# A gated mix of linear attention and a token MLP on one core: eight accumulators in the first stage, bias columns turned on VectorE, w2's second half moved in the load queue, kv in four column groups

## The chip, the cores and the metric

The kernel runs on one core of one Trainium2 chip. The metric is the device time of one execution in microseconds (us). Before the change it is 163.13 us, the median of three runs from 163.01 to 163.31.

## What is computed

The input x has 2048 rows (tokens) of 512 features, all arrays are bf16. With 32 heads of 16 features the reference is, cut to what matters:

```python
qkv = (x @ wqkv) split into q, k, v per head
phi = lambda t: where(t > 0, t + 1, exp(t)) + 1e-6
pq, pk = phi(q), phi(k)
kv  = einsum("bhsd,bhse->bhde", pk, v)          # 16x16 per head
den = einsum("bhqd,bhd->bhq", pq, pk.sum(over s)) + 1e-6
a   = (pq @ kv / den) @ wo
h   = layernorm(x)                              # over the features
u   = gelu(einsum("bsd,sf->bdf", h, w1) + b1)   # mixes tokens, 2048 -> 1792
b   = (einsum("bdf,fs->bds", u, w2) + b2), transposed
g   = sigmoid((x * gate_w).sum(-1))
out = g * a + (1 - g) * b
```

The output is divided through by the gate: with odds = exp(x . gate_w), out = (odds * a + b) / (1 + odds), so both halves can be summed in one accumulator.

## The kernel before, in words

The tokens are 16 tiles of 128 rows (t), the features 4 blocks of 128 (k, j), the hidden width of the MLP 14 blocks of 128 (NF). PSUM is one pool of eight banks, each 128x512 in fp32; every accumulator takes one. TensorE's order is the order of the program, and so are SP's queue, VectorE's and ScalarE's instructions that stand in `pin` or `keep_in_program_order`.

1. **Start** (lines 133 to 186). SP's queue loads x and the first part of w1 (w1A, one row block per token tile) in turns. ScalarE's queue loads the bias rows (b1 as 14 rows, b2 as 16) and the first 128 columns of w1A. TensorE runs 18 warm-up products of ones and then turns the bias rows into columns with an identity matrix (vps); ScalarE copies these out at t = 1 (L229, L230).
2. **Stage one** (L216 to L277). VectorE does the LayerNorm of a tile and TensorE multiplies it into NFA = 7 accumulators accA, row block after row block; the last four row blocks are done accumulator by accumulator, so that ScalarE can apply gelu to each. VectorE then does the gate sums of 12 tiles (L253).
3. **k** (L314). For each tile four matmuls k = x wk, phi on ScalarE and VectorE (L280), and, four tiles behind, four matmuls that sum G = x^T phi(k) in four banks (g_step). VectorE adds up z, the sum of phi(k), beside that.
4. **The mixed stage** (L469 to L491). Seven more blocks of the MLP's first layer (accB, from w1's second part w1B) stand between the q-tiles (L347), the block-diagonal kv product (kv_blocks, L416) and its product with wo (w2_blocks, L436). z makes a way through DRAM: zp_dram, transposing loads, a reduction (z_row), zr_dram, and back to all partitions (z_mixed); z_order puts it in order in zb.
5. **Normalisation** (normalise, L388). Per tile VectorE multiplies phi(q) by z, reduces, inverts and scales by odds and the inverse, in four operations. SP stores the tile in q_dram; after each four tiles, turn (L408) loads them back transposed into pqT, 512 columns, in four transposing loads (one per feature block).
6. **Output** (L538 to L556). For 8, then 4, then 3 tiles TensorE first sums the MLP's second layer into held accumulators yps (y_mm, 14 matmuls of w2h and uT) and then adds the attention part (a_mm, four matmuls of pqT and W2sb); finish scales by 1/(1+odds) and adds the bias on ScalarE, and SP stores. The last tile is done in 384 and 128 columns, the first on VectorE, the last on ScalarE.

w2 comes in two halves of 1024 columns. Half 0 takes the place of w1A (wpool has two equal buffers), half 1 that of w1B, which is read until the last accB matmul. Each of SP's loads and stores is issued when its data and its place are there and all before it in SP's queue have been issued:

```python
for t in range(12):
    normalise(t)              # ends with: store tile t to q_dram
    if t == 3:
        for f0, f1 in ((0, 3), (3, 7), (7, 10), (10, NF)):
            load_w2(1, f0, f1 - f0)
    if t % 4 == 3:
        turn(t // 4)          # four transposing loads of these four tiles
```

Before a transposing load of q_dram is issued, the four stores that it reads must have landed.

Of the kernel before, what the change touches and what calls it, by code (L numbers as in the profile page):

```python
# [7 lines left out]

ACT = mybir.ActivationFunctionType
ALU = mybir.AluOpType  # L10
# [1 line left out]
BF16 = mybir.dt.bfloat16  # L12
# [4 lines left out]
def kernel(  # L17
# [13 lines left out]
    nc = tc.nc  # L31
    P = nc.NUM_PARTITIONS
# [7 lines left out]
    S, D = X.shape  # L40
    F = B_w1.shape[1]
    NT = S // P
    ND = D // P
    NF = F // P
    SC = 512
    NSC = S // SC
    assert S == 2048 and D == 512 and F == 1792
    NFA = NF // 2
    FA = NFA * P
    TAIL = 4  # L50

# [5 lines left out]
    b1_view = B_b1.rearrange("(f p) -> f p", p=P)  # L57
    b2_view = B_b2.rearrange("(t p) -> t p", p=P)
    gw_row_view = gate_w.rearrange("(o d) -> o d", o=1)

    persist = ctx.enter_context(tc.tile_pool(name="persist", bufs=1))
    wpool = ctx.enter_context(tc.tile_pool(name="wstream", bufs=2))
    work = ctx.enter_context(tc.tile_pool(name="work", bufs=3))
    dpool = ctx.enter_context(tc.tile_pool(name="dpool", bufs=1, space=bass.MemoryType.DRAM))
    psum = ctx.enter_context(tc.tile_pool(name="psum", bufs=8, space=bass.MemoryType.PSUM))
# [1 line left out]
    def ptile(shape, dt, name):  # L67
        return persist.tile(shape, dt, name=name, tag=name)

    def bank(name):  # L70
        return psum.tile([P, SC], FP32, name=name, tag="bank")

    def mm(o, lhsT, rhs, start, stop, **kw):
        tc.keep_in_program_order(
            nc.tensor.matmul(o, lhsT=lhsT, rhs=rhs, start=start, stop=stop, **kw)  # L75
        )
# [5 lines left out]
    wk_sb = ptile([P, ND, D], BF16, "wk_sb")  # L82
    wv_sb = ptile([P, ND, D], BF16, "wv_sb")
    wo_sb = ptile([P, ND, D], BF16, "wo_sb")
    pqT = ptile([P, ND, S], BF16, "pqT")
    uT = ptile([P, NF, D], BF16, "uT")
    G_sb = ptile([P, ND, D], BF16, "G_sb")
    kvbdT = ptile([P, ND, P], BF16, "kvbdT")
    pq = ptile([P, NT, D], BF16, "pq")
    zb = ptile([P, D], FP32, "zb")  # L90
# [2 lines left out]
    prod = ptile([P, NH, HEAD + 1], FP32, "prod")  # L93
    W2sb = ptile([P, ND, D], BF16, "W2sb")
    mask = ptile([P, P], BF16, "mask")
    ident = ptile([P, P], BF16, "ident")
    gw_b = ptile([P, D], BF16, "gw_b")
    b_rows = ptile([NF + NT, P], BF16, "b_rows")
    b1_sb = ptile([P, NF], FP32, "b1_sb")
    b2_sb = ptile([P, NT], FP32, "b2_sb")  # L100
    mv = ptile([P, NT, nc.vector.BN_AGGR_DIM], FP32, "mv")
# [11 lines left out]
    eps_t = ptile([P, 1], FP32, "eps_t")  # L113

    nc.vector.memset(eps_t[:], EPS)


    w1A = wpool.tile([P, NT, FA], BF16, name="w1A", tag="w")
    w1B = wpool.tile([P, NT, FA], BF16, name="w1B", tag="w")

    pin = tc.keep_in_program_order

    def load(o, i, eng=None, **kw):
        pin((eng or nc.sync).dma_start(out=o, in_=i, **kw))  # L124

    def load_x(t0, t1):
        load(xr[:, t0:t1, :], x_view[:, t0:t1, :])

    def load_w1a(t):
        load(w1A[:, t, :], w1_view[:, t, 0:FA])  # L130


    tbl = work.tile([P, 1], FP32, name="tbl", tag="tbl", bufs=2)
    load(b_rows[0:NF, :], b1_view, nc.scalar)
    load(w1A[:, 0, 0:P], w1_view[:, 0, 0:P], nc.scalar)
    load(b_rows[NF : NF + NT, :], b2_view, nc.scalar)
    pin(nc.scalar.activation(out=tbl[:], in_=eps_t[:], func=ACT.Sqrt))

    load_x(0, 1)
# [2 lines left out]
    for t in range(1, NT):  # L142
        if t + 1 < NT:
            load_x(t + 1, t + 2)
        load_w1a(t)
    load(gw_b[:], gw_row_view.to_broadcast([P, D]))
    load(wk_sb[:], wqkv_view[:, :, D : 2 * D])
    for c in range(NSC):
# [11 lines left out]
    for j in range(ND):  # L160
# [4 lines left out]
    load(wq_sb[:], wqkv_view[:, :, 0:D])  # L165


    make_identity(nc, ident[:])
    nc.gpsimd.memset(mask[:], 0.0)
    nc.gpsimd.affine_select(  # L170
        out=mask[:], in_=mask[:], compare_op=ALU.is_gt, fill=1.0,
# [3 lines left out]
        out=mask[:], in_=mask[:], compare_op=ALU.is_ge, fill=0.0,  # L175
# [6 lines left out]
    one = nc.const_aps.tensor(1.0, [P, 256], BF16)  # L182
    for _ in range(18):
        mm(warm_ps[:, :256], one[:, 0:P], one, True, True)
    vps = bank("vps")
    mm(vps[:, : NF + NT], b_rows[:], ident[0 : NF + NT, 0 : NF + NT], True, True)

    BS = nc.vector.BN_STATS_DIM  # L190
# [2 lines left out]
    def ln_bn(t, d0, d1, h, parts):  # L193
        if h == 0:
            stats[t] = work.tile([P, parts, BS], FP32, name="stats", tag=f"stats{parts}", bufs=4)
        pin(nc.vector.bn_stats(out=stats[t][:, h, :], in_=xr[:, t, d0:d1]))  # L196
# [9 lines left out]
    def ln_apply(t):  # L206
        pin(nc.vector.reciprocal(out=rstd[:, t : t + 1], in_=sd[:, t : t + 1]))
        pin(
            nc.vector.tensor_scalar(
                out=xh[:, t, :], in0=xr[:, t, :],  # L210
                scalar1=mv[:, t, 0:1], scalar2=rstd[:, t : t + 1],
                op0=ALU.subtract, op1=ALU.mult,
            )
        )
# [4 lines left out]
    for t in range(1, NT):  # L219
        if t < HALVES:  # L220
            ln_bn(t, 0, D // 2, 0, 2)
            ln_apply(t - 1)
            ln_bn(t, D // 2, D, 1, 2)
        else:
            ln_bn(t, 0, D, 0, 1)
            ln_apply(t - 1)
        ln_aggr(t)
        if t == 1:
            pin(nc.scalar.copy(out=b1_sb[:], in_=vps[:, :NF]))  # L229
            pin(nc.scalar.copy(out=b2_sb[:], in_=vps[:, NF : NF + NT]))  # L230
    ln_apply(NT - 1)


# [31 lines left out]

    accA = [bank("accA") for _ in range(NFA)]

    def mlp1(acc, w, col, t, last):
        mm(acc[:], w[:, t, col : col + P], xh[:, t, :], t == 0, last)

    for t in range(NT - TAIL):
        for j in range(NFA):
            mlp1(accA[j], w1A, j * P, t, False)
    for j in range(NFA):
        for t in range(NT - TAIL, NT):
# [49 lines left out]
    def evict(o, acc, i):  # L325
        if i % 2 == 0:
            pin(nc.scalar.copy(out=o, in_=acc))
        else:
            pin(nc.vector.tensor_copy(out=o, in_=acc))

    for i in range(ND):
        evict(G_sb[:, i, :], Gps[i][:], i)
    pin(nc.vector.tensor_copy(out=z_parts[:, 0, :], in_=zacc[:]))
# [2 lines left out]
            out=z_parts[:, 1, :], in0=zacc[:], in1=z_parts[:, 0, :], op=ALU.subtract  # L336
# [4 lines left out]
    def mlp1_block(j):  # L341
        acc = bank("accB")
        for t in range(NT):
            mlp1(acc, w1B, (j - NFA) * P, t, t == NT - 1)
        return acc
# [70 lines left out]
    def kv_blocks():  # L416
        kvps = bank("kvps")
        for j in range(ND):
            for k in range(ND):
                for p in range(0, P, 64):  # L420
                    c = j * P + p
                    mm(kvps[p : p + 64, j * 64 : j * 64 + 64], wv_sb[:, k, c : c + 64],
                       G_sb[:, k, c : c + 64], k == 0, k == ND - 1, tile_position=(0, p))

        for j in range(ND):
            for p in range(0, P, 32):
                r = (p + 32 * j) % P
                pin(
                    nc.vector.tensor_tensor(
                        out=kvbdT[r : r + 32, j, p : p + 32],  # L430
                        in0=kvps[p : p + 32, j * 64 + p % 64 : j * 64 + p % 64 + 32],
                        in1=mask[p : p + 32, p : p + 32], op=ALU.mult,
                    )
                )
# [12 lines left out]
    w2s = []  # L447

    def load_w2(h, f0, n=7):
        if f0 == 0:  # L450
            w2s.append(wpool.tile([P, NF, S // 2], BF16, name="w2h", tag="w"))
        load(
            w2s[h][:, f0 : f0 + n, :],
            w2_view[:, f0 : f0 + n, h * (S // 2) : (h + 1) * (S // 2)],
        )
# [10 lines left out]
    gates = [[], [12, 13], [14, 15], []]  # L466
    qi = 0
    waiting = []
    for b in range(NFA):  # L469
        acc = mlp1_block(NFA + b)  # L470
        waiting.append((acc, NFA + b))
        if b == 0:
            kv_blocks()
        if b == 1:
            w2_blocks()
        if b < QB:
            for _ in range(n_q[b]):
                q_tile(qi)
                qi += 1
            for t in gates[b]:  # L480
                gate(t)
            if b == 2:
                gate_odds(0, NT)
            if b == 1:
                z_row()
        if b == QB - 1:
            z_order()
        if b >= QB - 1:
            for a, j in waiting:
                gelu(a, j)  # L490
            waiting = []  # L491
# [7 lines left out]

    for t in range(12):  # L500
        normalise(t)
        if t == 3:
            for f0, f1 in ((0, 3), (3, 7), (7, 10), (10, NF)):
                load_w2(1, f0, f1 - f0)
        if t % 4 == 3:
            turn(t // 4)
# [12 lines left out]

    def finish(t, yps, d0, d1):  # L520
        ot = work.tile([P, D], BF16, name="ot", tag="ot", bufs=6)
        if t < NT - 1 or d1 == D:
            pin(
                nc.scalar.activation(  # L524
                    out=ot[:, d0:d1], in_=yps[:, d0:d1], func=ACT.Identity,
                    scale=c1[:, t : t + 1], bias=c2[:, t : t + 1],
                )
            )
        else:
            pin(  # L530
                nc.vector.tensor_scalar(  # L531
                    out=ot[:, d0:d1], in0=yps[:, d0:d1], scalar1=c1[:, t : t + 1],
                    scalar2=c2[:, t : t + 1], op0=ALU.mult, op1=ALU.add,
                )
            )
        load(o_view[:, t, d0:d1], ot[:, d0:d1])
# [14 lines left out]
    t = NT - 1  # L551
# [35 lines left out]
```

## Time and profile before

| what | value |
|---|---|
| median of the runs | 163.13 us |
| the profiled execution | 163.22 us |
| its span, first to last instruction | 161.5 us |
| granted TensorE clock | 1.0 |
| TensorE, VectorE, ScalarE busy | 98%, 73%, 33% |
| 128x512 matmul of accB, busy for 16 | 3.45 us |
| HBM read, written | 19.28 MB, 4.46 MB |

The profile is of one execution. Its times count from the start of the span, and the 1.7 us between span and execution time lie outside it. Matmuls are pipelined: a matmul's own duration (379 ns for 512 columns) is longer than the 0.216 us from one start to the next. The chain of waits goes back from the last instruction, at each step to what released it. "Landing" is the moment at which a transfer has signalled its end; SP's line shows only the time in which it issues. All loads and stores that this document speaks of go through queue q1 (SP's) but for those issued by ScalarE, which go through q10.

### The profile page before, as it was taken

Reading aid. Unit: us, or ns where it says so; the run is one execution under the profiler, and the core shown is the slowest. Engines: PE = TensorE matmul, PEld = TensorE weight load, DVE = VectorE, ACT = ScalarE, POOL = GpSimd, SP = SyncE. Lnnn points to the kernel's source line nnn. Section 1 sums busy time; section 2 is a strip of 40 time slices with the busy share of each in tenths; the row PEclk is TensorE's granted clock in tenths of the full one; section 3 lists DMA queues with packets and bytes.
Section 4 is the critical chain, followed back from the end, with each engine's and each line's share of the span. In section 5 each row is a group of like instructions: output and inputs, shape, how many; then the busy total and the mean of one; then the engine's idle time right before and its main releaser. Section 6 shows DMA issues by size and latency. Waiting matters only on the chain.

```text
span 161.5 us, 2209 instructions
## 1 busy us (share of the span) xinstructions
PE 157.6 (98%) x789; PEld 72.9 (45%) x789; DVE 117.1 (73%) x271; ACT 53.6 (33%) x92; POOL 1.6 (1%) x10
## 2 busy tenths in 40 slices
PE   7999999999999999999999999999999999999992
PEld 5344444444444445444444444444444444444452
DVE  2899989999999996998959999999999900000001
ACT  4222248962342124261448720000008321150041
POOL 3000000000000000000000000000000000000000
PEclk9999999999999999999999999999999999999999
DMA  4999996445799742179930103999565367260021
GB/s 129 277 349 354 320 234 130 99 101 106 236 394 375 188 131 81 38 210 383 332 65 0 38 33 85 318 396 299 159 79 162 80 187 252 65 180 19 0 97 32
DMA packets 36838, 28.33 MB, mean 175 GB/s; under 512 B 20444, under 2 KB 33116, under 8 KB 36828
## 3 DMA queue, kind: packets, MB, share of 16 engines
q1 hardware_dynamic: 36352, 27.90, 58.7%
q10 hardware_dynamic: 476, 0.30, 0.6%
q8 instruction: 6, 0.10, 0.3%
q14 instruction: 4, 0.03, 0.1%
HBM read 19.28 MB, written 4.46 MB: 147 GB/s over the span
## 4 chain that ended last, share of the span: by engine, by line
PE 94%; DMA 3%; SPq 1%; ACT 0%; issue 0%; ACTq 0%
PE yps L75 39%; PE accB L75 15%; PE accA L75 14%; PE qacc L75 9%; PE Gps L75 9%; PE kacc L75 9%; DMA w1A<-in_B_w_dram 3%; SPq L124 1%; PE kvps L75 0%; ACT ot L524 0%; PE w2ps L75 0%; ACTq L524 0%
## 5 line engine op out<-in xcount | busy, mean ns | idle before, releaser
L75 PE MATMUL yps<-uT,w2h 128*128 128x512 bf16 (+2 forms) x238 | 49.2, 366 | 0.0
L75 PEld LDWEIGHTS <-w2h 128*128 128x128 bf16 x238 | 22.8, 98 | 25.9
L524 ACT ACTIVATE ot<-yps,c,c 128x512 bf16<-128x512 f32 (+1 forms) x16 | 12.0, 758 | 50.0 <-DVE pq L400 24.4
L75 PE MATMUL accB<-xh,w1B 128*128 128x512 bf16 x112 | 25.0, 379 | 0.0
L75 PE MATMUL accA<-xh,w1A 128*128 128x512 bf16 x112 | 24.5, 379 | 0.2 <-DMA w1A<-in_B_w_dram 0.2
L531 DVE TENSOR_SCALAR ot<-yps,c,c 128x384 bf16<-128x384 f32 x1 | 0.7, 677 | 28.7 <-PE yps L75 28.7
L75 PEld LDWEIGHTS <-xT 128*128 128x128 bf16 x128 | 12.3, 98 | 14.9 <-issue 0.2
L75 PEld LDWEIGHTS <-w1B 128*128 128x128 bf16 x112 | 10.9, 98 | 13.2
L75 PEld LDWEIGHTS <-w1A 128*128 128x128 bf16 x112 | 10.8, 98 | 13.4 <-DMA w1A<-in_B_w_dram 0.7
L75 PE MATMUL kacc<-wk_sb,xT 128*128 128x512 bf16 x64 | 15.8, 379 | 0.0
L75 PE MATMUL Gps<-pk,xr 128*128 128x512 bf16 x64 | 15.8, 379 | 0.0
L75 PE MATMUL yps<-W2sb,pqT 128*128 128x512 bf16 (+2 forms) x68 | 14.6, 366 | 0.0
L75 PE MATMUL qacc<-wq_sb,xT 128*128 128x512 bf16 x64 | 14.5, 379 | 0.0
L282 ACT ACTIVATE e<-qacc 128x512 bf16<-128x512 f32 x16 | 9.6, 597 | 12.2 <-PE qacc L75 8.0
L282 ACT ACTIVATE e<-kacc 128x512 bf16<-128x512 f32 x16 | 9.2, 598 | 12.7 <-DVE pk L289 6.8
L196 DVE BATCH_NORM_STATS2 stats<-xr 128x6 f32<-128x512 bf16 (+1 forms) x19 | 11.0, 581 | 2.2 <-DMA xr<-in_A_x_dram 2.0
L400 DVE SCALAR_TENSOR_TENSOR pq<-pq,odds,rd 128x512 bf16<-128x512 bf16 x16 | 12.0, 752 | 0.6
L396 DVE TENSOR_REDUCE den<-prod 128x32 f32<-128x544 f32 x16 | 11.5, 720 | 0.6
L289 DVE SCALAR_TENSOR_TENSOR pk<-kacc,e 128x512 bf16<-128x512 f32 x16 | 11.1, 692 | 1.0
L289 DVE SCALAR_TENSOR_TENSOR pq<-qacc,e 128x512 bf16<-128x512 f32 x16 | 11.1, 691 | 0.6
L241 DVE CUSTOM_DVE_ANT_0 junk<-xr,gw_b 128x512 bf16<-128x512 bf16 x16 | 11.0, 690 | 0.5
L284 DVE TENSOR_SCALAR e<-e 128x512 bf16<-128x512 bf16 x32 | 9.2, 287 | 2.8 <-ACT e L282 2.4
(54 smaller groups left out, 95.3 us busy)
## 6 DMA issues: line engine op xcount, KB each, us to landing
w1B<-in_B_w_dram SPq DMA_DIRECT2D x4, 896.0 KB, 7.1
w2h<-in_B_w_dram SPq DMA_DIRECT2D x2, 1792.0 KB, 7.8
w1A<-in_B_w_dram SPq DMA_DIRECT2D x15, 224.0 KB, 4.3
xr<-in_A_x_dram SPq DMA_DIRECT2D x16, 128.0 KB, 3.9
q_dram<-pq SPq DMA_DIRECT2D x16, 128.0 KB, 1.8
w2h<-in_B_w_dram SPq DMA_DIRECT2D x2, 1024.0 KB, 11.2
out_dram<-ot SPq DMA_DIRECT2D x15, 128.0 KB, 1.8
w2h<-in_B_w_dram SPq DMA_DIRECT2D x2, 768.0 KB, 7.1
```

Source lines behind the costliest of these rows:

```text
L75: nc.tensor.matmul(o, lhsT=lhsT, rhs=rhs, start=start, stop=stop, **kw)
L124: pin((eng or nc.sync).dma_start(out=o, in_=i, **kw))
L196: pin(nc.vector.bn_stats(out=stats[t][:, h, :], in_=xr[:, t, d0:d1]))
L241: nc.vector.tensor_tensor_reduce(out=junk[:], in0=xr[:, t, :], in1=gw_b[:], scale=1.0, scalar=0.0, op0=ALU.mult, op1=ALU.add, accum_out=gp ...
L282: pin(nc.scalar.activation(out=e[:], in_=acc[:], func=ACT.Exp))
L284: nc.vector.tensor_scalar(out=e[:], in0=e[:], scalar1=1.0, scalar2=PHI_EPS, op0=ALU.min, op1=ALU.add)
L289: nc.vector.scalar_tensor_tensor(out=o, in0=acc[:], scalar=0.0, in1=e[:], op0=ALU.max, op1=ALU.add)
L396: pin(nc.vector.tensor_reduce(out=den[:], in_=prod[:], op=ALU.add, axis=AX.X))
L400: nc.vector.scalar_tensor_tensor(out=heads, in0=heads, scalar=odds[:, t : t + 1], in1=rd[:].unsqueeze(2).to_broadcast([P, NH, HEAD]), op0= ...
L524: nc.scalar.activation(out=ot[:, d0:d1], in_=yps[:, d0:d1], func=ACT.Identity, scale=c1[:, t : t + 1], bias=c2[:, t : t + 1],)
L531: nc.vector.tensor_scalar(out=ot[:, d0:d1], in0=yps[:, d0:d1], scalar1=c1[:, t : t + 1], scalar2=c2[:, t : t + 1], op0=ALU.mult, op1=ALU.add,)
```

## The change

Stage one gets eight blocks instead of seven and the mixed stage six instead of seven, so w1A has 1024 columns and w1B 768; the two now have a pool tag each. The bias rows are loaded on SP's queue behind row block 4, into a tile that GpSimd cleared, and are turned in the LayerNorm loop at t = 8 by four 32x32 transposes on VectorE, with two copies to fp32; the identity, the vps product and ScalarE's copies go. The four loads of w2's second half move from behind the store of q-tile 3 to behind that of q-tile 0. kv is computed in products of 32 columns on four column groups instead of 64 on two. G_sb takes the place of wk_sb, which was read for the last time before. The last 128 columns of the output are finished on VectorE.

```diff
-    NFA = NF // 2
+    NFA = 8
...
-    b_rows = ptile([NF + NT, P], BF16, "b_rows")
+    b_rows = ptile([32, P], BF16, "b_rows")
+    b_cols = ptile([P, 32], BF16, "b_cols")
...
+    nc.gpsimd.memset(b_rows[:], 0.0)
-    w1A = wpool.tile([P, NT, FA], BF16, name="w1A", tag="w")
-    w1B = wpool.tile([P, NT, FA], BF16, name="w1B", tag="w")
+    w1A = wpool.tile([P, NT, FA], BF16, name="w1A", tag="w1st")
+    w1B = wpool.tile([P, NT, F - FA], BF16, name="w1B", tag="w2nd")
...
-    load(b_rows[0:NF, :], b1_view, nc.scalar)
     load(w1A[:, 0, 0:P], w1_view[:, 0, 0:P], nc.scalar)
-    load(b_rows[NF : NF + NT, :], b2_view, nc.scalar)
...
         load_w1a(t)
+        if t == 4:
+            load(b_rows[0:NF, :], b1_view)
+            load(b_rows[NF : NF + NT, :], b2_view)
...
-    make_identity(nc, ident[:])
...
-    vps = bank("vps")
-    mm(vps[:, : NF + NT], b_rows[:], ident[0 : NF + NT, 0 : NF + NT], True, True)
...
-        if t == 1:
-            pin(nc.scalar.copy(out=b1_sb[:], in_=vps[:, :NF]))
-            pin(nc.scalar.copy(out=b2_sb[:], in_=vps[:, NF : NF + NT]))
+        if t == NT // 2:
+            for p in range(0, P, 32):
+                pin(nc.vector.transpose(out=b_cols[p : p + 32, :], in_=b_rows[:, p : p + 32]))
+            pin(nc.vector.tensor_copy(out=b1_sb[:], in_=b_cols[:, 0:NF]))
+            pin(nc.vector.tensor_copy(out=b2_sb[:], in_=b_cols[:, NF : NF + NT]))
...
+    G_sb = persist.tile([P, ND, D], BF16, name="G_sb", tag="wk_sb")
...
-                for p in range(0, P, 64):
+                for p in range(0, P, 32):
                     c = j * P + p
-                    mm(kvps[p : p + 64, j * 64 : j * 64 + 64], wv_sb[:, k, c : c + 64],
-                       G_sb[:, k, c : c + 64], k == 0, k == ND - 1, tile_position=(0, p))
+                    mm(kvps[p : p + 32, j * 32 : j * 32 + 32], wv_sb[:, k, c : c + 32],
+                       G_sb[:, k, c : c + 32], k == 0, k == ND - 1, tile_position=(0, p))
...
-            w2s.append(wpool.tile([P, NF, S // 2], BF16, name="w2h", tag="w"))
+            w2s.append(wpool.tile([P, NF, S // 2], BF16, name="w2h", tag=("w1st", "w2nd")[h]))
...
-    for b in range(NFA):
+    for b in range(NF - NFA):
...
-        if t == 3:
+        if t == 0:
             for f0, f1 in ((0, 3), (3, 7), (7, 10), (10, NF)):
                 load_w2(1, f0, f1 - f0)
...
-        if t < NT - 1 or d1 == D:
+        if t < NT - 1:
```

## The prediction

> **What bounds the kernel now.** I read the page's engine table first, then the chain of waits in order of time, then the timeline around the few places where that chain leaves TensorE, and last the timeline of SP's queue with the landings of its transfers.
>
> ```profile
> PE 157.6 (98%) x789; PEld 72.9 (45%) x789; DVE 117.1 (73%) x271; ACT 53.6 (33%) x92; POOL 1.6 (1%) x10
> ...
> PE 94%; DMA 3%; SPq 1%; ACT 0%; issue 0%; ACTq 0%
> ```
>
> TensorE works 98% of the 161.5 us span and is 94% of the chain. In the chain in order of time:
>
> ```profile
> 2.67 4.09 DMA w1A<-in_B_w_dram
> 6.76 0.05 issue
> 6.80 22.84 PE accA L75 x105
> ...
> 60.72 0.62 PE kvps L75 x32
> ...
> 96.45 62.22 PE yps L75 x306
> ```
>
> The chain waits for w1A's second row block (issued 2.67, landed 6.76); from 6.80 to 158.67 it is TensorE without a hole, one 128x512 matmul every 0.216 us (16 of accB in 3.45). So only three things can shorten it: what precedes 6.80, the number and price of the matmuls, and the tail after 158.67. Only a wait of TensorE can lengthen it. Where a wait is near, SP's queue shows:
>
> ```profile
> 99.18 2.13 SPq L124 DMA_DIRECT2D w2h<-in_B_w_dram  x4
> 101.49 10.29 SPq L124 DMA_TRANSPOSE pqT<-q_dram  x4
> 111.89 1.98 SPq L124 DMA_DIRECT2D q_dram<-pq  x4
> 115.39 6.00 SPq L124 DMA_TRANSPOSE pqT<-q_dram  x4
> 121.44 2.04 SPq L124 DMA_DIRECT2D q_dram<-pq  x4
> ```
>
> The columns are start, length and count. The second group of transposes (columns 512 to 1023 of pqT) begins at 115.39, and in the trace its four land at 117.92, 121.38, 121.76 and 123.23. TensorE starts the a-products of tile 0 at 120.47, so tile 4, the first that needs this group, takes its fourth slice 19 matmuls later, at 124.57. The margin is 1.3 us: the smallest in the kernel.
>
> **Eight banks in the first stage.** The matmuls stay 224 in all (8+6 blocks for 7+7). In the trace the seventh accA matmul starts at 6.234 and the eighth at 6.804, a hole of 0.35 us over the pitch, while w1A's row block 1 is awaited. An eighth block fills it with one matmul, worth 0.216, if that block lands as before. It is 256 KB instead of 224 and the one ahead of it 224 instead of 192: per DMA engine 16 packets that grow by 256 bytes. By the 2048-byte packets (about 0.084 us each in the trace) that is some 0.17 us; the bias rows' 30 packets leave this stretch and give a little back. Net gain 0 to 0.216; I take **0.10**. Removing the vps product (0.17) lies inside the same wait and adds nothing.
>
> Later row blocks have slack: x and w1A land a pair per 0.95 us now, about 1.05 then, against eight matmuls in 1.73. The two bias loads take two places on SP's queue (0.4 us each); w1A's block 5 was 3 us early. On VectorE four 32x32 transposes and two copies cost at most 6 x 0.19 (the 32x32 products of L429 are 187 ns) = 1.1 us; a LayerNorm tile takes 1.17 against TensorE's 1.73, so they hide, and without that cover they would cost 1.1.
>
> **The shift.** Stage one is 3.45 us longer (16 matmuls), the two blocks after the q-tiles that much shorter. Everything between, the phi(q) and the normalisation on VectorE included, comes 3.2 us later against the start of yps (3.45 less the gains). VectorE's gates end at 32.33 and phi of the first k-tile starts at once; then it waits some 2 us instead, so the shift isn't caught up. Normalise(7), stored from 108.85 on, is then ready at 112.1. The loads behind stage one (w1A is 512 KB larger, 1.4 us at 360 GB/s) move less than their use.
>
> **kv on four column groups.** 64 products of 32 columns replace 32 of 64. In the trace a pair of column groups starts every 31.7 ns, 16 pairs in 0.50 us, with 0.13 to the next matmul. There are again 16 rounds, of four. If the round goes by columns (27 of its 31.7 ns are 64 columns at 0.216 us for 512), 16 x 13.3 = 0.21 is gained; if it has a fixed price, nothing; if each product keeps its 15.8 ns, 64 make 1.01 and 0.51 is lost. The nearest row, the w2ps products on 32x32 positions, start 3.3 ns apart, so issue allows a round of four in 13 ns. I take **0.15** gained, between the first two, and keep -0.51 to 0.21. The Trainium skill, "TensorE: Matmul & The Clock Gate", section "Wait — 56ns, not 53.3ns?", says that matmuls never start closer than about 25 ns however small they are: by it 64 would take 1.6 us, 1.1 more than now, and the time would be 1.2 above my sum. The trace disagrees for products in different groups, which start 3.3 ns apart.
>
> **Tail.** The last 128 columns go from ScalarE (460 ns) to VectorE, whose 384 columns took 677; at about 1.04 ns a column (512 columns of CAST 686, 32 columns 187) 128 make 0.41. Between 0.3 and 0.46; I take 0.04 gained. VectorE is free from 158.43 on.
>
> The gains add up to 0.10 + 0.15 + 0.04 = 0.29.
>
> **w2's second half behind the first store.** This is the step that decides. The 3.67 MB move past the stores of q-tiles 1, 2 and 3 on SP's queue. They don't start at store 0 (91.2 + 3.3), because they go into w1B's place and wait for the last accB matmul: 96.45 - 0.25 = 96.2. Stores 1 to 3 are queued behind this wait and then behind the transfer itself. The price of being behind such a transfer is a row of this page:
>
> ```profile
> zr_dram<-z_cols SPq DMA_DIRECT2D x1, 2.0 KB, 5.9
> ```
>
> 2 KB take 5.9 us to land: issued at 75.79 behind w2's first half (68.55), their packets run only from 79.8, when the 2048-byte packets stop. Now step by step.
> - From w2's first issue to its last landing: 99.18 to 111.97, 12.8 us now; from w2's first half to zr_dram's landing 13.2. So 96.25 + 12.8 = 109.05.
> - Stores 1 to 3 behind it, 128 KB each, 24 packets of 44 ns per engine in all (1.5 at most, by 0.5 us each in the trace): 1.1, so 110.15. Before, all four stores had landed by 100.5, and the first transposes were issued while w2 still ran (101.49 to 111.78), so that they landed right behind it, at 113.85. In the changed kernel the first transpose waits for store 3.
> - Four transposes issued: 5.03 when clean (125.01 to 130.04), 6.00 in the group above.
> - Stores 4 to 7 and their landing to the second group's first transpose: 111.78 to 115.39 and 121.40 to 125.01, 3.61 both times.
> - That to the fourth landing: 6.52 when clean (125.01 to 131.53), 7.84 above.
>
> The 6.00 and 7.84 have a common cause in the trace: a 16 KB instruction packet (queue q8) at 119.38, with data packets of 1.3 us around it. These packets come at 20.30, 47.83, 66.25, 90.78, 119.38 and 146.42, each time after 227 to 264 matmuls and weight loads. 62 more such instructions (64 for kv, 2 fewer for vps) bring the fifth forward by 31 x 0.216 = 6.7 us, to about 112.5: among the first transposes. It then costs 0.97 there (6.00 for 5.03) and none in the second group. The Trainium skill ("Runtime: NRT & Kernel Launch", section "Instruction fetch mechanics") has blocks of 16 KiB, 256 instructions, which agrees with these counts, and calls their cost mostly hidden: by that 0.97 is left out.
>
> Sum: 110.15 + 6.00 + 3.61 + 6.52 = 126.3 for the fourth slice, against 124.57 - 0.25 = 124.3: TensorE stands **2.0 us** in front of tile 4's last a-product. Bounds: without the fetch and with the shortest terms (109.0 + 1.0 + 5.03 + 3.61 + 6.52 = 125.2) 0.9; with 13.2 and 1.5 as well as the fetch 127.1, so 2.8. Group one itself lands at about 117.5 and is needed at 120.2: no wait. Everything after tile 4 is late by the same stall and has more slack: group three, begun 3.5 later, lands at 135 against 139.5 + 1.6, group four at 147.5 against 152 + 1.6.
>
> The profiled execution took 163.22 (span 161.5). 163.22 - 0.29 + 2.0 = 164.9; the median shown is 0.09 below that execution, so **164.8 us**.
>
> **Rivals.**
> 1. No stall. The mechanism would be that stores 1 to 3 overtake w2's packets (each lands 1.7 us after its issue when alone); then the first transposes are issued while w2 runs, land behind it at about 111, the second group starts near 114.6, 1.5 us before it is needed. Then the gains alone: 163.13 - 0.29 = 162.8, faster. It decides from store 3 landing 2 us earlier than in my sum. Against it stands the row of 5.9. Chance 0.14, half of it beyond the bound of 0.2%, which is about what a measurement of this kernel can tell from no change.
> 2. The stall without the fetch's 0.97, 0.9 to 1.2 us: 163.7 to 164.0. It decides if the instruction packet falls between the two groups. Chance 0.22.
> 3. The kv products keep 15.8 ns each: 0.51 lost for 0.15 gained. TensorE moves w2's start along, so the stall stays: 163.13 - 0.14 + 0.51 + 2.0 = 165.5. The 3.3 ns speak against it. [...] Chance 0.04.
> 4. The larger first row blocks land so late that stage one starves (a pair per 1.73 or slower): nothing near it in the trace; 0.02, up to 166.
>
> The forecast proper has 0.53; what I did not see, 0.05. Faster: 0.07 from rival 1 and 0.03 of the unseen, 0.10; same: 0.07 and 0.02, 0.09; slower 0.81. The range 163.4 to 165.7 leaves out rivals 1 and 4 and the unseen and takes in both bounds of the stall (163.13 - 0.29 + 0.9 = 163.7, + 2.8 = 165.6) and of kv beside a middling one.
>
> **What would show it.** Right: a gap of TensorE of 1 to 2.8 us some 4 us after the a-products begin, ended by DMA pqT; w2 issued at about 96.2; stores 1 to 3 with landings of 7 to 11 us; the second transposes near 119 to 120. kvps in 0.40 to 0.63 us, the first accA hole below 0.2. Wrong: stores 1 to 3 landing within 3 us, or no wait before tile 4; a gap of TensorE in stage one or before kvps would be a cause that I missed.

## The result and the profile after

The changed kernel takes 164.35 us, the median of ten runs from 163.62 to 165.39, against 163.31 (163.01 to 163.70) for the kernel before in ten runs beside it. The ratio is 1.0066, 95% interval 1.0038 to 1.0094: slower by about 1.0 us. The forecast was 164.8, in a range of 163.4 to 165.7. The profiled execution took 164.17, and its span is 162.4.

On the page, the engines' row and the chain's shares by engine:

```profile
PE 157.3 (97%) x820; PEld 72.8 (45%) x820; DVE 119.0 (73%) x278; ACT 53.1 (33%) x89; POOL 1.3 (1%) x9
...
PE 71%; DVE 19%; DMA 4%; SPq 2%; issue 1%; ACT 1%; DVEq 0%
```

TensorE was 94% of the chain and is 71%. The list of what TensorE waited for (us in total, times, longest) gives the reason. Before the change it is:

```profile
PE warm_ps L75 <- PEq L571: 0.8, 1, 0.8
PE accA L75 <- DMA w1A<-in_B_w_dram: 0.2, 1, 0.2
```

After the change it is:

```profile
PE yps L74 <- DMA pqT<-q_dram: 1.0, 1, 1.0
PE warm_ps L74 <- PEq L571: 0.8, 1, 0.8
PE accA L74 <- DVE xh L205: 0.4, 1, 0.4
```

The wait of yps for pqT is new. It stands in TensorE's timeline behind the 19th a-product:

```profile
120.24 4.26 PE L74 MATMUL yps<-W2sb,pqT 128*128 128x512 bf16 x19
125.54 1.69 PE L74 MATMUL yps<-W2sb,pqT 128*128 128x512 bf16 x7 [1.03 <-DMA pqT<-q_dram]
```

The list counts from the end of a matmul, which is modelled. In the trace the starts on both sides are 124.122 and 125.536, 1.41 apart instead of 0.216: 1.20 us are lost. The stalls below are taken from the starts in the same way. SP's queue in the same stretch:

```profile
94.39 0.33 SPq L123 DMA_DIRECT2D q_dram<-pq  x1
96.26 2.49 SPq L123 DMA_DIRECT2D w2h<-in_B_w_dram  x4
98.85 3.46 SPq L123 DMA_DIRECT2D q_dram<-pq  x3
109.49 5.71 SPq L123 DMA_TRANSPOSE pqT<-q_dram  x4
115.30 1.98 SPq L123 DMA_DIRECT2D q_dram<-pq  x4
118.78 5.03 SPq L123 DMA_TRANSPOSE pqT<-q_dram  x4
```

Three stores are issued by 102.3, and then SP stands until 109.49: they land at 108.69, 109.00 and 109.34, behind w2 (last landing 108.32). The second group starts at 118.78 instead of 115.39.

The chain now runs back through the normalisation (DVE 19%), and that track is wrong. It leaves SP's queue here:

```profile
116.39 0.45 DVE pq L401
116.84 1.83 DMA q_dram<-pq
```

The columns are start, length and what. The store that starts at 116.84 is tile 7's. In the trace tile 7 was normalised by 112.07, and the store was issued when the three stores ahead of it had been. The multiplication at 116.39 belongs to a later tile. A releaser is inferred; it is checked by the time at which the data was ready.

Four terms account for 0.92 of the 0.95 us between the two profiled executions: the stall +1.20, stage one -0.20 (k's first matmul at 32.73 instead of 29.48, 16 matmuls of 0.216 later), kv -0.03, the tail -0.05.

### The profile page after: what moved, and what is told of

It reads as the page before. It is cut to its first block, busy times and chain, and to the rows that moved or that the text cites. A ratio compares the mean times of both kernels' runs of the same rounds, so it can differ in the third digit from the quotient of the medians.

```text
span 162.4 us, 2272 instructions
## 1 busy us (share of the span) xinstructions
PE 157.3 (97%) x820; PEld 72.8 (45%) x820; DVE 119.0 (73%) x278; ACT 53.1 (33%) x89; POOL 1.3 (1%) x9
## 4 chain that ended last, share of the span: by engine, by line
PE 71%; DVE 19%; DMA 4%; SPq 2%; issue 1%; ACT 1%; DVEq 0%
PE yps L74 21%; PE accA L74 17%; PE Gps L74 9%; PE accB L74 9%; PE kacc L74 9%; PE qacc L74 7%; DVE den L397 4%; DVE pq L401 4%; DVE prod L392 4%; SPq L123 2%; DVE rd L399 2%; DVE pq L288 2%; DMA pqT<-q_dram 2%; DMA xr<-in_A_x_dram 1%; DMA q_dram<-pq 1%
## 5 line engine op out<-in xcount | busy, mean ns | idle before, releaser
L74 PE MATMUL accA<-xh,w1A 128*128 128x512 bf16 x128 | 27.8, 379 | 0.4 <-DVE xh L205 0.4
L524 ACT ACTIVATE ot<-yps,c,c 128x512 bf16<-128x512 f32 x15 | 11.6, 777 | 48.1 <-PE yps L74 40.3
L74 PE MATMUL accB<-xh,w1B 128*128 128x512 bf16 x96 | 21.5, 379 | 0.0
L531 DVE TENSOR_SCALAR ot<-yps,c,c 128x384 bf16<-128x384 f32 (+1 forms) x2 | 1.1, 544 | 26.7 <-PE yps L74 26.7
L74 PEld LDWEIGHTS <-w1A 128*128 128x128 bf16 x128 | 12.5, 98 | 15.6 <-DMA w1A<-in_B_w_dram 0.9
L74 PEld LDWEIGHTS <-w1B 128*128 128x128 bf16 x96 | 9.4, 98 | 11.3
```

What stands on the lines that cost most here:

```text
L524: nc.scalar.activation(out=ot[:, d0:d1], in_=yps[:, d0:d1], func=ACT.Identity, scale=c1[:, t : t + 1], bias=c2[:, t : t + 1],)
```

## The experiments

My theory: w2's transfer stands ahead of stores 1 to 3 in one queue, their landing holds the first transposes, and these hold the second group. Rivals: the later normalisation is the cause, or the DMA engines' load, or the slow group of transposes alone. Each run was made beside runs of the kernel before, whose medians were 163.18 to 163.42.

| run | median us | ratio to before, 95% interval |
|---|---|---|
| w2 behind store 3, rest as changed | 165.45 | 1.0126 (1.0105 to 1.0146) |
| seven banks, rest as changed | 165.63 | 1.0130 (1.0110 to 1.0150) |
| w2 on ScalarE's queue | 163.12 | 0.9987 (0.9974 to 1.0000) |
| 40 more TensorE instructions | 163.55 | 1.0014 (1.0000 to 1.0027) |
| half of w2 ahead | 163.07 | 0.9995 (0.9983 to 1.0008) |
| seven banks, bias late | 165.29 | 1.0126 (1.0109 to 1.0142) |
| w2 and bias rows on ScalarE's queue | 163.08 | 0.9994 (0.9983 to 1.0006) |
| before, with the move alone | 164.13 | 1.0039 (1.0021 to 1.0057) |
| half of w2 ahead, more warm-up | 163.33 | 0.9994 (0.9979 to 1.0009) |

**The move undone.**

```diff
-        if t == 0:
+        if t == 3:
             for f0, f1 in ((0, 3), (3, 7), (7, 10), (10, NF)):
```

> The changed kernel with w2's second half loaded behind store 3 again, all else as changed. Theory (queue order plus the later normalisation: with eight banks in stage one VectorE's normalisation is 3.2 us later against the start of yps, so store 3 goes at 102.0 and w2 follows it): from w2's first issue to the second group's first transpose the kernel before took 16.2 us (99.18 to 115.39), so 102.4 + 16.2 = 118.6 against 118.78 in the changed kernel. The stall before tile 4's last a-product stays at 0.9 to 1.5 us, and the time at 164.0 to 164.8, within 0.5 us of the changed kernel. Rival (moving w2 ahead of stores 1 to 3 is the whole cause): the second group starts near 115.4 as in the kernel before, no stall, 162.9 to 163.1.

It is 1.1 us slower than the changed kernel, not equal to it. The rival is out: the move is not the whole cause, it repairs part of another delay. My own theory had the mechanism and missed the size, since I expected 164.0 to 164.8. SP's queue:

```profile
95.00 7.92 SPq L123 DMA_DIRECT2D q_dram<-pq  x4
103.01 2.23 SPq L123 DMA_DIRECT2D w2h<-in_B_w_dram  x4
105.42 11.31 SPq L123 DMA_TRANSPOSE pqT<-q_dram  x4
116.83 1.99 SPq L123 DMA_DIRECT2D q_dram<-pq  x4
120.33 5.03 SPq L123 DMA_TRANSPOSE pqT<-q_dram  x4
```

Store 3 waits for the later normalisation, so w2 starts at 103.0, and the whole pattern of the kernel before (99.18 to 115.39) comes 3.8 to 4.9 later; two waits of TensorE lose 2.0 us. I had 118.6 for the second group. Of the miss of 1.7, 0.6 is w2's start. The other 1.1 comes with w2's transfer, 13.9 us from its issue to its last landing instead of 12.8, and with it the first group, 11.31 for 10.29. The 16 KB packet at 114.62 falls into this stretch; that it makes the difference is not shown.

**Seven banks, the move kept.**

```diff
-    NFA = 8
+    NFA = 7
```

> The changed kernel with seven blocks in stage one again, w2 behind store 0 and all else as changed. Theory (w2 waits for the last accB matmul at 96.4 whatever the split, and stores 1 to 3 lie behind its 3.67 MB in one queue): store 3 lands near 109.5, the second group starts at 118.8 to 119.5, and the stall is 0.9 to 1.6 us although VectorE is 3.2 us earlier; time 164.0 to 164.9. Rival (the 3.2 us by which the normalisation comes later is the whole cause): no stall, 163.1 to 163.3.

The stall stays, 1.05 us, although VectorE is early again: the rival is out. But the time is 0.7 above the top of the range that I expected, by waits in stage one:

```profile
PE accA L74 <- DVE xh L205: 1.3, 2, 0.7
PE yps L74 <- DMA pqT<-q_dram: 0.9, 1, 0.9
```

There VectorE's bias work (transposes and copies from 14.60 to 15.70) has no cover: the starts of the accA products lose 1.2 us in all, the last 0.85 of it near 24.

**The bias work behind the LayerNorm loop.** The same kernel with the block of transposes moved (its lines are shortened here):

```diff
-        if t == NT // 2:
-            (four transposes, two copies)
     ln_apply(NT - 1)
+    (four transposes, two copies)
```

> Seven blocks in stage one as in the run with seven banks, and the four bias transposes with their two copies moved behind the last LayerNorm tile. Theory (with seven blocks TensorE takes 1.51 us a tile, little more than VectorE's 1.18, and the 1.0 us of bias work in the loop makes TensorE catch up with LayerNorm near tile 12; the wait of 0.85 us there and smaller ones before are that): the holes of stage one go, the time falls by 0.8 to 1.3 us from 165.63 to 164.3 to 164.8, and what is left over the kernel before is the stall of the queue alone, 0.9 to 1.5 us. Rival (the holes come from the bias loads on SP's queue, which delay x): they stay, 165.3 to 165.8.

The holes in stage one go, so the rival about x's loads is out, and yet the time falls by only 0.3. The wait has moved, as TensorE's list of waits shows:

```profile
PE yps L74 <- DMA pqT<-q_dram: 0.9, 1, 0.9
PE Gps L74 <- DVE pk L286: 0.8, 1, 0.8
```

VectorE works almost without a pause from LayerNorm over the gates to the first phi(k), and with seven banks the first G product waits for the latter. So the 1.1 us of work costs TensorE 1.2 us at one place and 0.8 at the other. With eight banks and the work at t = 8 there is no such wait: they are what hides it.

**The move alone in the kernel before.** The diff is the one shown first, the other way round, on the old code.

> The kernel before with only the four loads of w2's second half moved from behind store 3 to behind store 0. Theory (the queue alone): w2 starts at 96.4 to 96.6, store 3 lands at 109 to 110.5, the second group starts at 118.5 to 119.8 and its fourth load lands at 125 to 126.5, against 124.57: a stall of 0.5 to 1.9 us and nothing else, 163.9 to 164.9. Rival (the move does no harm while the normalisation is early): no stall, 163.1 to 163.3.

The stall is there, with the order of the queue as the only change. SP's two groups, then TensorE's wait:

```profile
110.18 5.06 SPq L124 DMA_TRANSPOSE pqT<-q_dram  x4
...
118.84 5.19 SPq L124 DMA_TRANSPOSE pqT<-q_dram  x4
```

```profile
PE yps L75 <- DMA pqT<-q_dram: 0.5, 1, 0.5
```

TensorE's starts lose 0.71 us, and the median is 0.7 above the kernel before. The rival is out. The first group takes 5.06 here, so the stall doesn't need a slow group of transposes. With the first run this gives both causes singly: the move alone +0.7, the eight banks (with the small edits) under the old order +2.2, both +1.0.

**w2's second half on ScalarE's queue.**

```diff
             w2_view[:, f0 : f0 + n, h * (S // 2) : (h + 1) * (S // 2)],
+            nc.scalar if h else nc.sync,
```

> The changed kernel with the four loads of w2's second half issued by ScalarE instead of SP, at the same place of the program; the same bytes move at the same time, but not in SP's queue. Theory (waiting behind w2 in SP's queue is what delays stores 1 to 3): these land within about 2 to 4 us of their issue, the first transposes are issued from about 104 on and the second group well before 116; no stall, and the gains stay: 162.9 to 163.1, 1.2 us below the changed kernel. Rival (w2 takes the DMA engines themselves, so the stores wait for it in whatever queue it is): stores land at 107 or later, a stall of 0.5 us or more is left, 163.6 to 164.4.

No stall, 1.2 us below the changed kernel. The answer on DMA issues in a window around stores 2 and 3, first of the changed kernel, then of this run (count, KB each, median us to landing; the first is from 98.8 on and holds store 1 too):

```profile
q_dram<-pq SPq DMA_DIRECT2D x3, 128.0 KB, 9.4
```

```profile
q10 hardware_dynamic: 424, 0.84, 85.1%
q1 hardware_dynamic: 144, 0.13, 14.0%
...
q_dram<-pq SPq DMA_DIRECT2D x2, 128.0 KB, 5.2
```

In the trace stores 2 and 3 take 9.4 and 7.4 us behind w2, and 5.4 and 5.1 out of its queue, but not the 2 to 4 that I expected: w2 on q10 still holds 85% of the engines' time while the stores on q1 have 14%. So the rival is half right: store 3 lands at 107.02, as it said, yet no stall is left.

```profile
107.04 5.05 SPq L123 DMA_TRANSPOSE pqT<-q_dram  x4
...
116.36 5.03 SPq L123 DMA_TRANSPOSE pqT<-q_dram  x4
```

The second group starts 2.4 us earlier than in the changed kernel, and that is enough.

**Half of the bytes ahead.**

```diff
-            for f0, f1 in ((0, 3), (3, 7), (7, 10), (10, NF)):
+            for f0, f1 in ((0, 3), (3, 7)):
                 load_w2(1, f0, f1 - f0)
         if t % 4 == 3:
             turn(t // 4)
+        if t == 7:
+            for f0, f1 in ((7, 10), (10, NF)):
+                load_w2(1, f0, f1 - f0)
```

> The changed kernel with w2's second half cut in two: blocks 0 to 6 (1.83 MB) behind store 0 as in the change, blocks 7 to 13 behind the second group of transposes. All on SP's queue. Theory (the delay is the time of the bytes ahead in the queue): stores 1 and 2 land near 103.5 instead of 109, store 3 at about 104, the first transposes start there, the second group when tile 7 is normalised and stored, at 114 to 115; it lands by 121 to 122, no stall. The other blocks land by 127 and are needed from 128.5 on. Time 162.9 to 163.2. Rival (any w2 load ahead of the stores costs the stall, because SP waits for w1B's place): 164.0 or more.

The theory held in its order, and every step came somewhat later than I wrote: stores 1 to 3 land at 104.70, 105.06 and 105.39 (1.2 to 1.6 later) and the second group starts at 115.58 (0.6 behind the range). The other blocks land by 128.92 instead of 127. There is still no stall. With half of the bytes ahead the first transposes start 4.1 us earlier than in the changed kernel:

```profile
105.41 5.05 SPq L123 DMA_TRANSPOSE pqT<-q_dram  x4
...
115.58 5.04 SPq L123 DMA_TRANSPOSE pqT<-q_dram  x4
```

**The packet moved.** Twenty products more in front of kv, whose sums are overwritten by the real ones:

```diff
         kvps = bank("kvps")
+        for _ in range(5):
+            for p in range(0, P, 32):
+                mm(kvps[p : p + 32, 0:32], wv_sb[:, 0, p : p + 32], G_sb[:, 0, p : p + 32],
+                   True, True, tile_position=(0, p))
```

> The changed kernel with 20 more kv products ahead of kv (the first four of kv five times, their sums are overwritten by the real ones): 40 TensorE instructions, 0.1 to 0.2 us of TensorE. Theory (a 16 KB instruction packet comes every 256 TensorE instructions and holds up transposing loads that run beside it): the packet of 111.7 moves 4.3 us forward to about 107.5, into w2's own transfer; the first group of transposes is then issued in 5.0 us instead of 5.7, the second starts 0.5 to 0.8 earlier, the stall falls from 1.2 to 0.5 to 0.8, time 0.3 to 0.6 below the changed kernel in the profile. Rival (the packet and the slow transposes only coincide): 5.7 stays and the time rises by 0.1 to 0.2.

The kernel with more work is 0.8 us faster than the changed one. The 16 KB packet comes at 109.24 instead of 111.68 and falls into the pause before the transposes:

```profile
96.80 2.16 SPq L123 DMA_DIRECT2D w2h<-in_B_w_dram  x4
...
109.94 5.04 SPq L123 DMA_TRANSPOSE pqT<-q_dram  x4
115.09 1.99 SPq L123 DMA_DIRECT2D q_dram<-pq  x4
118.59 5.03 SPq L123 DMA_TRANSPOSE pqT<-q_dram  x4
```

The first group takes 5.04 instead of 5.71; from w2's issue to the second group it is 21.8 us instead of 22.5. TensorE comes to tile 4 later by 0.54, and the stall is 0.2 for 1.2. The packet moved 2.4, not 4.3; why is open (w2 still filled the engines until 108.7). All runs of this kernel lie within 0.93 us, those of the changed one within 1.77; that the packet makes the larger spread is likely and not shown.

**Two attempts at the start.** The first adds to the run with ScalarE's queue the bias loads as they were, ahead of and behind w1A's first 128 columns:

```diff
+    load(b_rows[0:NF, :], b1_view, nc.scalar)
     load(w1A[:, 0, 0:P], w1_view[:, 0, 0:P], nc.scalar)
+    load(b_rows[NF : NF + NT, :], b2_view, nc.scalar)
...
-        if t == 4:
-            load(b_rows[0:NF, :], b1_view)
-            load(b_rows[NF : NF + NT, :], b2_view)
```

> The run with w2's second half on ScalarE's queue, and the bias rows loaded on ScalarE's queue again, around w1A's first 128 columns as in the kernel before. Theory (in the changed kernel these columns, issued at 0.80 instead of 1.49, share the DMA engines with x's first tile, which lands at 3.06 to 3.10 in five profiles against 2.94; LayerNorm and the first accA product follow it): x lands at 2.94, the first accA product starts at 4.90 to 4.95 instead of 5.04, and the time falls by 0.1 to 162.9 to 163.1. Rival (w1A's second row block sets the pace of the start whatever x does, as in the kernel before): no change from 163.12 beyond 0.05.

x's first tile lands at 2.80 and the first accA product starts at 4.95, as expected, but the time stays (163.08 for 163.12). That fits the rival's number and lies at the upper end of the theory's; two such medians can't tell them apart. The rival's mechanism doesn't show either: w1A's second row block lands at 6.57, and no product waits for it. What stretches the start of this profile are the first four accA products, which start 0.38 to 0.43 us apart instead of 0.216. The second attempt adds the same edit and three warm-up products to the run with half of w2 ahead:

```diff
-    for _ in range(18):
+    for _ in range(21):
```

> The run with w2's second half cut in two, with the bias rows on ScalarE's queue as in the kernel before, and 21 instead of 18 warm-up products, so that TensorE's idle 0.5 us before the first accA product is filled. Theory (in three of eight profiles the first four to six accA products start 0.43 us apart, at half clock, after that idle stretch, and cost up to 0.8 us): they start 0.22 apart, the runs' spread shrinks and the median falls by 0.1 to 0.3 to 162.8 to 163.0. Rival (the clock's rise does not depend on that gap): no change, 163.0 to 163.1, or later by up to 0.2 where the added products delay the first accA product.

In its profile the first eight products do start 0.216 us apart, and yet there is no gain: 163.33 beside 163.42 for the kernel before, against 163.07 beside 163.18, and the runs spread over 1.1 us. That theory fell.

## Why the prediction was right, step by step

The forecast was a rise of 1.7 us (163.13 to 164.8), and 1.0 was measured. The stall came by the way that was forecast, but smaller.

- **w2 behind the first store**, the step that was to decide, did. Its chain as predicted and as found: w2's issue 96.25 and 96.26; store 3's landing 110.15 and 109.34; the first group 6.00 and 5.71; from there to the second group 3.61 and 3.58; its fourth landing 6.52 and 6.71 after that. So 126.3 became 125.49, and the stall 1.2 instead of 2.0. The mis-sized term is the way from w2's issue to store 3: 13.9 predicted, 13.1 measured. Nearly all of that is w2's own transfer, 12.8 us from issue to last landing before and 12.1 after; the stores added 1.0 where I had 1.1. In the five kernels with stores 1 to 3 queued behind the whole of it, it took 11.9 to 12.3, and 12.8 and 13.9 in the two where the first transposes were issued beside it. So the 12.8 was a row of another order; that the transposes are what lengthened it is likely and not shown.
- **The packet** was predicted at 112.5 among the first transposes and came at 111.68, with 5.71 for 5.03. With the packet moved away the group took 5.04. The Trainium skill ("Runtime: NRT & Kernel Launch", section "Instruction fetch mechanics") calls the cost of such a fetch mostly hidden. TensorE's own stream agrees: before the change it has no hole from 6.80 to 158.67, with six packets in that time. The transposing loads beside a packet pay all the same.
- **The shift of 3.2 us** was right in size (normalisation of tile 7 by 112.07 against 112.1), and the sum rightly left it out under the new order, where the store of tile 7 is issued only at 116.84. I did not see what the undone move shows: under the old order it would have cost 2.0 us. The move is a partial cure for the eight banks.
- **Stage one**: 0.10 gained predicted, 0.20 found, by another way. The hole before the eighth matmul is gone, but the first accA product starts at 5.05 instead of 4.93, since x's first tile lands at 3.10 instead of 2.94, beside w1A's first columns. The 0.20 is partly luck of this execution: in five profiles with this same stage one k's first matmul starts between 32.70 and 33.34, where 32.93 would be no gain.
- **The bias work** is hidden by the eighth block, as costed; without that cover it cost 1.2 and 0.8 in the two runs with seven banks (1.1 predicted).
- **kv**: 0.15 predicted, 0.03 found (first kv start to the next matmul, 0.627 before and 0.595 after). After a first gap of 39 ns the first eight rounds of four start 25 ns apart, the last eight 34; my 0.15 lay between 18 and 32 for all. The Trainium skill ("TensorE: Matmul & The Clock Gate", section "Wait — 56ns, not 53.3ns?") gives about 25 ns as the least distance of two starts. Between column groups this doesn't hold here, since products of one of the first eight rounds mostly start 2 to 5 ns apart; taken for each column group it agrees with these rounds.
- **Tail**: 0.41 us predicted, and the group's row says 410 ns for 460 of ScalarE:

```profile
L531 DVE TENSOR_SCALAR ot<-yps,c,c 128x128 bf16<-128x128 f32 x1 | 0.4, 410 | 0.3 <-PE yps L74 0.3
```

In the profiled pair the gains add up to 0.28, against 0.29 forecast. Over many runs they look smaller: the four kernels without the stall lie 0.1 to 0.2 us below their runs of the kernel before, each with an interval that reaches 1.0. In the medians each beats the changed kernel by 1.0 to 1.3 us, and none is clearly faster than the one before.

## What to carry to other kernels

Before a large load is moved forward in a queue, list what is issued behind it and when each of these is needed: a small store pays the whole remaining transfer, 7.4 to 9.8 us here, and what waits for its landing pays again. Where work is shifted between two stages, check the smallest margin in the later one: this one was 1.3 us and was spent twice, by the shift and by the order. A second queue or a load cut in two gave it back.

## What the runs showed of the hardware that was not expected

- Instructions arrive in 16 KB packets (queue q8), before the change one after every 226 to 264 of TensorE's matmuls and weight loads. In the eleven profiles the ten groups of four transposing loads of pqT with a packet in their midst took 5.6 to 6.1 us to issue. The others took 5.0 to 5.2, but for the two issued while w2 still ran in the same queue. Adding 40 instructions, which moved a packet, made a kernel 0.8 us faster.
- The first eight rounds of kv ran at 25 ns, the next at 34, and the run with 84 products broke at the same place, after 32 products: 64 instructions with their weight loads. From there on a weight load and its product take 8.4 ns together.
- In every profile TensorE starts at half its later rate: the warm-up products of 256 columns start 0.213 us apart, almost as far as products of 512 columns do later (0.216). This ends between 3.6 and 6.6 us. In four of eleven profiles it lasts into the first accA products, which then start 0.38 to 0.43 us apart, although the granted clock in the profile is 1.0 there. Filling the idle time before them did not change the times, and the two profiles with the longest idle time there (0.84 and 0.98 us) are not among the four. What sets the end is open.
